# Retuning the start of a planned RWKV-5 plus tanh-shrink kernel: when weights are fetched, where the own terms are made, and how wide the idle products are

## The chip, the cores and the metric

One core of a Trainium2 chip runs the whole program. The metric is the device time of one execution in microseconds (us), the median of three runs. A TensorE product of float32 appears in the trace as two passes, each a weight load (PEld) and a multiplication (PE); a transpose is one such pair.

## The reference

```python
state = zeros((B, H, D, D))                      # B=4, H=8, S=768, D=48
for t in range(S):
    cur = einsum('bhd,bhe->bhde', u[None] * k[t], v[t])
    y[t] = einsum('bhd,bhde->bhe', r[t], state + cur)
    state = w[None, :, :, None] * state + einsum('bhd,bhe->bhde', k[t], v[t])
x = y.transpose(0, 2, 1, 3).reshape(B * S, H * D)  # 3072 x 384
h = x @ w_in                                      # 384 x 2048
out = (h - tanh(h)) @ w_out                       # 2048 x 384
```

The recurrence is an attention with a decay `w` for each channel and a bonus `u` for a token's own term. The weights come as float64 and are handed over as 64-bit integers.

## The kernel before

**Attention.** The sequence is cut into 24 units of 64 steps of two batch entries (128 rows). For a unit the kernel loads r, k and v (`fetch`), transposes r and k on TensorE (`turn`), scales them by powers of the decay (`rT`, `kT`), multiplies k by r (`levels`), keeps what lies strictly below the diagonal with a predicated copy (`x.cp`), puts the own terms on the diagonal (`x.diag`), multiplies by v (`outputs`), updates the state (`to_state`, `keep`, `decay`) and evicts the result as the input `xt` of the dense part. Two units make one block of 256 tokens.

**Own terms.** For the first `OWN` units they are made on TensorE: ScalarE scales `kT` by decay and bonus (`own_k`), TensorE multiplies (`own_levels`, 16 products), and VectorE copies the diagonal with a predicate. For all later units VectorE multiplies r by k, multiplies by the bonus `ub` and sums (`own`, the line after it, `own_sum`: 3 instructions), and ScalarE writes eight scaled unit matrices (`diagonal`).

**Dense part.** A tile of 256 hidden columns needs 6 products of 128x256 (`h`), five activations, four VectorE instructions (`g`, `c1`, `c2`, `cp`, the last named L195 in the profile) and 8 products of 128x384 (`o`). The first six blocks go through the hidden columns in four passes, so that only a quarter of the weights is needed early.

**Weights.** Each piece of 768 KB (two w_in pieces, then two w_out pieces, and so on) is loaded into a staging tile `st` and turned into float32 by five VectorE and two ScalarE instructions (`convert`, L134 to L140). w_in pieces are loaded half by SyncE (two transfers of 288 KB) and half by GpSimd's queue (two of 96 KB); a w_out piece is one transfer of 768 KB. All r, k, v loads are SyncE transfers of 96 KB in runs of 192 bytes.

**The planner.** `Plan` fixes the order of every engine's instructions before the program is built. Each task has a cost, predecessors and a due time; `forward` lays them out in time, `backward` gives latest times, and `order` tries 600 random shifts of due times and keeps what ends sooner. Three of its models matter here. Transfers share a channel (`data` is the channel time of a transfer) and land some time after it. A weight transfer (`gated`) is not issued sooner than 45 us ahead of its due time. TensorE's instructions come in blocks (`CHUNK` 256 instructions, the first bound at 192); `ASKED` instructions into a block the next one is requested, and it comes `COMES` after that, or after what is already on the channel.

**Idle products.** While TensorE would wait, `filled` works out how many products of the identity with itself fit in the planned gap, and `order` puts them into the instruction stream. They compute nothing that is used; they keep TensorE's clock up. Their number is fixed in the program, so they run even if the gap turns out shorter.

```python
plan.fill = lambda to: T.matmul(to, ident, ident, start=True, stop=True), .25
```

Of the kernel before, what the change touches and what calls it, by code (L numbers as in the profile page):

```python
# [34 lines left out]
L = 2  # L35
FIRST = 6
PASSES = 4, 4, 4, 4
OWN = 4
SWAP = 2


# [190 lines left out]
class Plan:  # L232
# [5 lines left out]


    HOP, NEAR_HOP, LANDS, LANDED, LANES, EARLY, SPARE, WARM, SLOW = 0.16, 0.06, 2.4, 1.6, 8, 45.0, 20.0, 6.0, (60.0, 3.0)  # L240
    CHUNK, CHUNK_0, ASKED, COMES = 256, 192, 55, 3.0
    BEGIN = {"PE": 1.5, "DVE": 2.2, "ACT": 1.2, "POOL": 4.3, "SP": 1.2}

    def __init__(self):
        self.tasks, self.fill, self.fills = [], None, []

    def add(self, engine, cost, run, after=(), due=1e9, data=0, gated=False, steps=0):
        t = SimpleNamespace(engine=engine, cost=cost, run=run, after=[x for x in after if x], due=due, data=data,
# [16 lines left out]

    def forward(self, due):

        ready = [due[t.n] - self.EARLY if t.gated else 0.0 for t in self.tasks]
        count = [len(t.after) for t in self.tasks]
        waiting = self.queues(ready, count)  # L270
        free, lanes, channel = dict(self.BEGIN), {}, 0.0
        step, bound, comes, fills = 0, self.CHUNK_0, 0.0, iter(self.fills)
        filling = next(fills, None)
        starts, done, last, first, changed = [None] * len(ready), [], 0.0, {}, set(waiting)
        while len(done) < len(ready):
            for e in changed:
                ts = waiting[e]
                first.pop(e, None)
                if not ts:
                    continue  # L280
                start = max(free.get(e, 0.0), min(ready[x.n] for x in ts))
                t = min((x for x in ts if ready[x.n] <= start + 1e-9), key=lambda x: (due[x.n], x.n))
                if t.data:
                    start = max(start, lanes.setdefault(e, [0.0] * self.LANES)[0])
                else:

                    soon = [x for x in ts if ready[x.n] < start + t.cost and due[x.n] < due[t.n] - self.SPARE]
                    if soon:
                        t = min(soon, key=lambda x: (ready[x.n], x.n))
                        start = max(start, ready[t.n])  # L290
                first[e] = start, t
            e = min(first, key=lambda x: (first[x][0], x))
            start, t = first[e]
            waiting[e].remove(t)
            changed = {e}
            end = start + t.cost
            if e == "PE":
                if filling:
                    step += 4 * self.filled(filling, free[e], start, starts)
                    if t is filling[1]:  # L300
                        filling = next(fills, None)
                step += t.steps
                if step >= bound:
                    each = t.cost / max(t.steps, 1)
                    crossed = end - (step - bound) * each
                    late = max(0.0, comes - crossed)
                    end += late
                    comes = max(crossed + late + self.ASKED * each + .3, channel) + self.COMES
                    bound += self.CHUNK
            free[e] = end  # L310
            if t.data:
                channel = max(channel, start + 1.2) + t.data
                end = max(end + self.LANDS, channel + self.LANDED) + self.slow(start)
                lanes[e] = lanes[e][1:] + [end]
            starts[t.n] = start
            last = max(last, end)
            done.append(t)
            for x in t.then:
                ready[x.n] = max(ready[x.n], end + self.hop(t, x))
                count[x.n] -= 1  # L320
                if not count[x.n]:
                    waiting[x.engine].append(x)
                    changed.add(x.engine)
        return last, starts, done
# [4 lines left out]

    def filled(self, filling, free, start, starts):  # L330

        after = [starts[x.n] and starts[x.n] + x.cost + self.HOP for x in filling[0]]
        if None in after:
            return 0
        return max(0, int((start - max([free] + after)) / (self.fill[1] * (2 if start < self.WARM else 1))))

    def backward(self, plan):

# [27 lines left out]
    def order(self, tries=600):  # L366


        due = [t.due for t in self.tasks]
        for t in reversed(self.tasks):  # L370
            for x in t.then:
                due[t.n] = min(due[t.n], due[x.n] - t.cost - self.HOP - (self.LANDS if t.data else 0))
        plan = self.forward(due)
        for _ in range(4):
            due = self.backward(plan)
            plan = self.forward(due)
        chance = Random(3)
        for _ in range(tries):
            by, at, wide = chance.choice((0.3, 1, 2, 5)), chance.uniform(0, plan[0]), chance.choice((15, 40, 100, 700))
            moved = [x + chance.gauss(0, by) * (abs(start - at) < wide / 2) for x, start in zip(due, plan[1])]  # L380
            other = self.forward(moved)
            if chance.random() < .5:
                latest = self.backward(other)
                again = self.forward(latest)
                if again[0] < other[0]:
                    other, moved = again, latest
            if other[0] <= plan[0]:
                plan, due = other, moved
        self.due = due
        _, starts, done = plan  # L390
        free, order, fills = self.BEGIN["PE"], [], iter(self.fills)
        filling = next(fills, None)
        for t in done:
            t.start = starts[t.n]
            if t.engine == "PE" and filling:
                n = self.filled(filling, free, t.start, starts)
                order += [SimpleNamespace(engine="PE", cost=0.0, start=free, run=lambda to=filling[2]: self.fill[0](to))] * n
                if t is filling[1]:
                    filling = next(fills, None)
                free = t.start + t.cost  # L400
            order.append(t)
        return order
# [19 lines left out]
def near(ctx, tc, r, k, v, w, u, out, shared, weights):  # L422
# [84 lines left out]
    wcol = cols_ps[:, :NP]  # L507
    saved, w_u = fixed("saved", [128, 2 * NP]), fixed("w_u", [128, NP])
    idle, tab = (ps_d.tile([128, 2, d.NT], F32, name="h", tag="h") for _ in range(2))
    idle, tab = idle[:, 0, :128], tab.rearrange("s z t -> s (z t)")  # L510
    flat = "d p n -> d (p n)"

    def bounds():
# [7 lines left out]
            T.transpose(tab[:, p * 128 : (p + 1) * 128], twice[:, p].rearrange("d z n -> d (z n)"), ident)  # L521


    plan.fill = lambda to: T.matmul(to, ident, ident, start=True, stop=True), .25  # L524

    now = [add(e, 1.25 if e == "ACT" else .87, lambda e=e, at=at, x=x: e_of[e].dma_start(out=rows[at : at + NP, :, :D], in_=x.rearrange("(p i) d -> p i d", i=2)), due=-1, data=.05)
           for e, at, x in (("SP", 0, w), ("ACT", NP, u))]
# [8 lines left out]
    ups = add("ACT", .6, lambda: A.copy(w_up, power[:, :, None, :SHORT].to_broadcast([128, NP, 2, SHORT])), [now])  # L536
    now = add("DVE", 1.75, lambda: V.reciprocal(inverse, power), [now])
    doubled = add("DVE", .4, lambda: V.tensor_copy(twice, inverse[:, :, None, 1:].to_broadcast([128, NP, 2, SHORT])), [now])
    now = add("PE", .7, table, [doubled], steps=8)
    downs = add("ACT", .5, lambda: A.copy(w_down, tab.rearrange("s (h d) -> s h d", h=H)[:, :, :D]), [now])  # L540
    keeps = add("ACT", .2, lambda: A.copy(saved, cols_ps), [cols])
    w_us = add("DVE", .1, lambda: V.tensor_tensor(w_u, saved[:, :NP], saved[:, NP:], ALU.mult), [keeps])
# [21 lines left out]
    loads, converted = [], []  # L564
    for n in range(weights.count):

        queues, data = (("SP",), (2.4,)) if n % 4 > 1 else (("SP", "POOL") * 2, (.85, .55) * 2)
        of = [add(e, .55, lambda n=n, i=i, e=e: weights.load(n, i, e_of[e]), [converted[n - 4] if n >= 4 else None],
                  data=x, gated=True) for i, (e, x) in enumerate(zip(queues, data))]
        if weights.sources[n % 4 > 1].dtype != I64:  # L570
# [17 lines left out]
    def unit(n):  # L588
# [20 lines left out]
        def fetch(name, src, after):  # L609
            def run(z):  # L610
                if name == "k" and not hasattr(t, "kt"):
                    t.kt = first_k[slot] if direct else load.tile([128, H, D], F32, name="kt", tag="kt")
                to = {"r": rt, "v": vt}.get(name)
                Q.dma_start(out=(t.kt if to is None else to)[HALF[z], :, :D],  # L614
                            in_=src[half * 2 + z, :, steps_at, :].rearrange("h t d -> t h d"))

            of = [add("SP", .65, lambda z=z: run(z), after, data=.58) for z in range(2)]
            return add("none", 0, lambda: None, of)

        x.r = fetch("r", r, [b3.turn, b3.rk, b1.r])  # L620
# [18 lines left out]

        def own():  # L640
            t.rk = work.tile([128, H, D], F32, name="rk", tag="rk")
            V.tensor_tensor(t.rk, rt[:, :, :D], t.kt, ALU.mult)

        def own_sum():
            t.du = work.tile([128, H], F32, name="du", tag="du")
# [134 lines left out]
    def hidden(j, fs, f, due, pace):  # L780
# [8 lines left out]
        x.h = add("PE", 1.29, lambda: dense.h(t, 1), [now], due + 1.3, steps=12)  # L789
        last_h[j] = x.h  # L790
        if m == 0:
            plan.fills.append(([], now, idle))
        x.s = add("ACT", .48, lambda: dense.act(t, "s"), [x.h, b2.c1, b2.q, b2.small, b1.s])
        x.th = add("ACT", .48, lambda: dense.act(t, "th"), [x.h, b2.g, b1.th])
        x.tg = add("ACT", .48, lambda: dense.act(t, "tg"), [x.h, b2.cp, b1.tg])
        x.q = add("ACT", .63, lambda: dense.act(t, "q"), [x.s, b2.c2, b1.q])
        x.small = add("ACT", .63, lambda: dense.act(t, "small"), [x.s, b2.cp, b1.small])
# [3 lines left out]
        x.cp = add("DVE", .65, lambda: dense.vec(t, "cp"), [x.c2, x.small, x.g])  # L801
        now = add("PE", 1.3, lambda: dense.o(t, 0), [x.cp, converted[piece + 2], b1.o] + b1.empty + ([units[1].cp, units[1].diag] if m == 0 else []), due + 2 * pace, steps=8)
        if m == 0:
            plan.fills.append(([units[1].cp, units[1].diag], now, x_banks[1][:, 0, :128]))
        x.o = add("PE", 1.3, lambda: dense.o(t, 1), [now], due + 2 * pace + 1.3, steps=8)
        if not t.last:
            return
# [339 lines left out]
```

## Time and profile before

| | us |
|---|---|
| median of three runs | 622.67 |
| lowest, highest | 620.96, 622.95 |
| profiled span | 621.0 |
| TensorE busy | 602.6 |
| VectorE busy | 429.9 |
| ScalarE busy | 398.5 |
| products `h` (L165) and `o` (L203), busy | 281.6 and 280.6 |
| idle products (L524), busy, into `h` and into `x_ps` | 16.2 and 3.4 |

TensorE is busy for 97% of the span, but busy time of overlapping passes is counted from start to modelled end, and idle products count as busy. A time per instruction is therefore read from start to start.

### The profile page before, as it was taken

The page shows a single profiled execution, that of the slowest core. Times are in us where ns is not written, and L with a number is a line of the kernel's source. Part 1 is how long each engine was busy: PE and PEld are TensorE (multiplying, and loading weights), DVE is VectorE, ACT ScalarE, POOL GpSimd, SP SyncE. Part 2 cuts the span into 40 slices and gives each one's busy share as a digit, 9 for nine tenths or more (in the row PEclk, how much of TensorE's full clock was granted, in tenths as well). Part 3 has the DMA queues.
Part 4 walks back from the last instruction along what each step waited for, and adds up shares of the span by engine and source line. Part 5 has one row for each costly group of instructions (what it writes and reads, how often), then busy time and mean ns, then how long its engine had stood idle before and what let it go on. Part 6 is the DMA issues. An engine that isn't in the chain of part 4 may idle for free.

```text
span 621.0 us, 13303 instructions
## 1 busy us (share of the span) xinstructions
PE 602.6 (97%) x5337; PEld 448.6 (72%) x5337; DVE 429.9 (69%) x700; ACT 398.5 (64%) x873; POOL 68.8 (11%) x153
## 2 busy tenths in 40 slices
PE   7799999999999999999999999999999999999995
PEld 6777777677777777777777777777777777777773
DVE  5699979998985797776676747475766455455552
ACT  2488879978665667555574756674774566665651
POOL 4001311300000000011132010011010101110100
PEclk9799999999999999999999999999999999999998
DMA  8976796234520000011233111211210100100101
GB/s 124 201 131 112 128 219 117 45 74 132 91 98 0 1 1 2 0 26 39 52 84 63 29 33 27 51 35 23 55 31 3 27 14 8 26 5 4 26 1 31
DMA packets 86320, 33.71 MB, mean 54 GB/s; under 512 B 78536, under 2 KB 80680, under 8 KB 86248
## 3 DMA queue, kind: packets, MB, share of 16 engines
q1 hardware_dynamic: 81084, 25.57, 21.1%
q0 software_dynamic: 4992, 6.99, 5.2%
q8 instruction: 44, 0.72, 0.5%
q10 hardware_dynamic: 172, 0.20, 0.1%
q14 instruction: 28, 0.23, 0.1%
HBM read 26.94 MB, written 4.72 MB: 51 GB/s over the span
## 4 chain that ended last, share of the span: by engine, by line
PE 84%; DVE 5%; DMA 4%; ACT 3%; issue 2%; SPq 1%; POOL 0%; POOLq 0%; DVEq 0%; ACTq 0%
PE h L165 37%; PE o L203 36%; PE yk_ps L584 5%; PE x_ps L626 3%; DMA rt<-in_r_dram 2%; PE x_ps L584 1%; PE h L524 1%; DMA xt<-rest 1%; SPq L614 1%; DVE rT L630 1%; DMA st<-in_moe_w_in_dram 1%; ACT kT L638 1%; DVE tg L193 1%; DVE g L195 1%; DVE at L761 0%
## 5 line engine op out<-in xcount | busy, mean ns | idle before, releaser
L203 PE MATMUL o<-w_out_sb,g 128*128 128x384 f32 x768 | 280.6, 489 | 1.8 <-DVE g L195 1.2
L165 PE MATMUL h<-xt,w_in_sb 128*128 128x256 f32 x1152 | 281.6, 381 | 0.0
L165 PEld LDWEIGHTS h<-xt,w_in_sb 128*128 128x128 f32 x1152 | 216.1, 190 | 62.3
L203 PEld LDWEIGHTS o<-w_out_sb,g 128*128 128x128 f32 x768 | 142.6, 190 | 65.4 <-DVE g L195 1.5
L191 DVE SCALAR_TENSOR_TENSOR tg<-s,tg 128x512 f32<-128x512 f32 x96 | 66.0, 688 | 71.0 <-ACT tg L178 44.1
L189 DVE TENSOR_TENSOR g<-h,th 128x512 f32<-128x512 f32 x96 | 65.9, 686 | 50.3 <-ACT s L174 31.7
L174 ACT ACTIVATE s<-h 128x512 f32<-128x512 f32 x96 | 57.1, 595 | 54.2 <-PE h L165 54.1
L178 ACT ACTIVATE tg<-h 128x512 f32<-128x512 f32 x96 | 57.0, 594 | 53.7 <-PE h L165 53.6
L176 ACT ACTIVATE th<-h 128x512 f32<-128x512 f32 x96 | 57.3, 597 | 38.6 <-PE h L165 38.6
L195 DVE COPY_PREDICATED g<-small,tg 128x512 f32<-128x512 int32 x96 | 70.4, 734 | 5.6
L193 DVE SCALAR_TENSOR_TENSOR tg<-q,tg 128x512 f32<-128x512 f32 x96 | 65.9, 686 | 7.2 <-ACT q L180 4.4
L180 ACT ACTIVATE q<-s,m1b 128x512 f32<-128x512 f32 x96 | 69.7, 726 | 0.5
L182 ACT ACTIVATE small<-s,smallb 128x512 f32<-128x512 f32 x96 | 69.6, 725 | 0.1
L726 POOL DMA_DIRECT2D xt<-rest x66 | 32.2, 495 | 202.1 <-ACT rest L712 201.3
L650 ACT ACTIVATE at<-same,du 128x64 f32<-128x64 f32 x160 | 41.3, 339 | 0.4
L226 POOL DMA_DIRECT2D out_dram<-part x24 | 12.5, 527 | 157.8 <-DVE part L211 157.8
L630 DVE TENSOR_TENSOR rT<-x_ps,w_up 128x512 f32<-128x512 f32 x24 | 16.5, 689 | 16.8 <-ACT kT L638 10.4
L638 ACT COPY kT<-x_ps 128x512 f32<-128x512 f32 x22 | 12.9, 587 | 20.3 <-PE x_ps L626 14.7
L211 DVE TENSOR_TENSOR part<-o,part 128x384 f32<-128x384 f32 x36 | 19.8, 549 | 6.4 <-PE o L203 6.4
L584 PEld LDWEIGHTS yk_ps<-at,vt 64*64 64x64 f32 x752 | 13.4, 137 | 11.2 <-issue 4.4
L226 POOL DMA_DIRECT2D out_dram<-o x20 | 10.6, 533 | 95.7 <-ACT o L220 95.5
L524 PE MATMUL h<-ident 128*128 128x128 f32 x90 | 16.2, 336 | 4.8 <-issue 3.3
(96 smaller groups left out, 442.0 us busy)
## 6 DMA issues: line engine op xcount, KB each, us to landing
st<-in_moe_w_out_dram SPq DMA_DIRECT2D x8, 768.0 KB, 10.6
rt<-in_r_dram SPq DMA_DIRECT2D x48, 96.0 KB, 3.5
vt<-in_v_dram SPq DMA_DIRECT2D x48, 96.0 KB, 3.1
st<-in_moe_w_in_dram SPq DMA_DIRECT2D x16, 288.0 KB, 5.4
kt<-in_k_dram SPq DMA_DIRECT2D x44, 96.0 KB, 3.3
out_dram<-part POOLq DMA_DIRECT2D x24, 96.0 KB, 2.2
out_dram<-o POOLq DMA_DIRECT2D x20, 96.0 KB, 2.1
st<-in_moe_w_in_dram POOLq DMA_DIRECT2D x16, 96.0 KB, 4.6
```

The costliest lines, as they stand in the source:

```text
L165: self.nc.tensor.matmul(t.h2[:, z], self.w_in_sb[:, t.f // 2, kk, z * 128 : (z + 1) * 128], self.xts[t.j][:, kk].rearrange("p b t -> p (b ...
L174: A.activation(out, t.h, AF.Square)
L176: A.activation(out, t.h, AF.Tanh)
L178: A.activation(out, t.h, AF.Tanh, scale=G1)
L180: A.activation(out, t.s, AF.Square, bias=self.m1b)
L182: A.activation(out, t.s, AF.Relu, bias=self.smallb, scale=-1.0)
L189: V.tensor_tensor(t.g, t.h, t.th, ALU.subtract)
L191: V.scalar_tensor_tensor(t.tg, t.s, C4, t.tg, ALU.mult, ALU.mult)
L193: V.scalar_tensor_tensor(t.tg, t.q, K1, t.tg, ALU.add, ALU.mult)
L195: V.copy_predicated(t.g, t.small.bitcast(I32), t.tg)
L203: self.nc.tensor.matmul(self.outs[i], t.g2[:, z, i * C : (i + 1) * C], self.w_out_sb[:, t.f + z, :], start=t.first and z == 0, stop=t.last ...
L584: T.matmul(*args, skip_group_check=True, **how)
```

## The change

It has four parts. (1) `FIRST` = 9.5: weight transfers are planned no sooner than 9.5 us, which puts them behind the loads of the first two units. (2) The planner gets larger figures for transfers and for the arrival of an instruction block. (3) `OWN` goes from 4 to 1: only the first unit has its own terms made on TensorE. (4) An idle gap is filled with 128x512 products (`ident` by the decay powers `w_up`) as far as they fit and with 128x128 ones for the rest; those need `w_up`, so a first stretch of narrow ones up to the task `tabled` is kept. The other edits follow from these: `first_k` tiles are wider than 48 columns, hence the slice in `own`, and they share their buffers with `th`, hence the two extra predecessors of `x.th`.

```diff
-OWN = 4
+OWN = 1
-    CHUNK, CHUNK_0, ASKED, COMES = 256, 192, 55, 3.0
+    CHUNK, CHUNK_0, ASKED, COMES, FIRST = 256, 192, 55, 3.4, 9.5
-        ready = [due[t.n] - self.EARLY if t.gated else 0.0 for t in self.tasks]
+        ready = [max(self.FIRST, due[t.n] - self.EARLY) if t.gated else 0.0 for t in self.tasks]
-                    step += 4 * self.filled(filling, free[e], start, starts)
+                    step += 4 * len(self.filled(filling, free[e], start, starts))
-        return max(0, int((start - max([free] + after)) / (self.fill[1] * (2 if start < self.WARM else 1))))
+        runs = []
+        for cost, run in filling[2]:
+            n = max(0, int((start - free) / (cost * (2 if start < self.WARM else 1))))
+            free += n * cost
+            runs += [run] * n
+        return runs
...
-    plan.fill = lambda to: T.matmul(to, ident, ident, start=True, stop=True), .25
+    def fills(to):
+        wide = w_up.rearrange("d p z t -> d (p z t)")
+        return [(.9, lambda: T.matmul(to, ident, wide, start=True, stop=True)),
+                (.25, lambda: T.matmul(to[:, :128], ident, ident, start=True, stop=True))]
...
-        queues, data = (("SP",), (2.4,)) if n % 4 > 1 else (("SP", "POOL") * 2, (.85, .55) * 2)
+        queues, data = (("SP",), (3.0,)) if n % 4 > 1 else (("SP", "POOL") * 2, (1.2, .8) * 2)
-            of = [add("SP", .65, lambda z=z: run(z), after, data=.58) for z in range(2)]
+            of = [add("SP", .65, lambda z=z: run(z), after, data=.62) for z in range(2)]
-            V.tensor_tensor(t.rk, rt[:, :, :D], t.kt, ALU.mult)
+            V.tensor_tensor(t.rk, rt[:, :, :D], t.kt[:, :, :D], ALU.mult)
-            plan.fills.append(([], now, idle))
+            plan.fills += [([], tabled, fills(idle)[1:]), ([ups], now, fills(idle))]
-        x.th = add("ACT", .48, lambda: dense.act(t, "th"), [x.h, b2.g, b1.th])
+        x.th = add("ACT", .48, lambda: dense.act(t, "th"), [x.h, b2.g, b1.th] + ([units[m].rk, units[m].kw] if m < L else []))
-            plan.fills.append(([units[1].cp, units[1].diag], now, x_banks[1][:, 0, :128]))
+            plan.fills.append(([units[1].cp, units[1].diag], now, fills(x_banks[1][:, 0])))
```

What the planner makes of it at the start, engine by engine. SyncE: before, the order was r, k, v of the first unit, one w_in transfer, r and k of the second, two w_in, v of the second, w_in, w_out, then r and k of the third and the bonus; now k, r, v of the first unit, the bonus, k, r and half of v of the second, two w_in, the rest of v, k and r of the third, two w_in, w_out. GpSimd's four w_in transfers, which stood ahead of its first copy out of `v`, now stand behind it. TensorE: the transpose of the second unit's k now precedes the first unit's own-term product, where it followed the first unit's outputs. Between the second unit's `levels` and the first `o` product there stand 11 wide and 9 narrow idle products, where there were 18 narrow into `h` and 12 narrow into `x2_ps`. The `levels` of the fifth unit now stand ahead of the first `o`. VectorE and ScalarE: 3 VectorE and 8 ScalarE instructions for the own terms of units two, three and four each, in place of one and four. The second w_out piece is loaded later, between the halves of the v of the sixth unit, where it stood ahead of the v of the third. Over the whole program the changes between `h` and `o` are about as many as before (304 against 309).

More of the change, by code (lines that the diff above doesn't have):

```diff
@@ L240 @@
     HOP, NEAR_HOP, LANDS, LANDED, LANES, EARLY, SPARE, WARM, SLOW = 0.16, 0.06, 2.4, 1.6, 8, 45.0, 20.0, 6.0, (60.0, 3.0)
-    CHUNK, CHUNK_0, ASKED, COMES = 256, 192, 55, 3.0
+    CHUNK, CHUNK_0, ASKED, COMES, FIRST = 256, 192, 55, 3.4, 9.5
     BEGIN = {"PE": 1.5, "DVE": 2.2, "ACT": 1.2, "POOL": 4.3, "SP": 1.2}
     def __init__(self):
-        self.tasks, self.fill, self.fills = [], None, []
+        self.tasks, self.fills = [], []
     def add(self, engine, cost, run, after=(), due=1e9, data=0, gated=False, steps=0):
@@ L330, in filled @@
     def filled(self, filling, free, start, starts):
-        after = [starts[x.n] and starts[x.n] + x.cost + self.HOP for x in filling[0]]
-        if None in after:
-            return 0
-        return max(0, int((start - max([free] + after)) / (self.fill[1] * (2 if start < self.WARM else 1))))
+        for x in filling[0]:
+            if starts[x.n] is None:
+                return []
+            free = max(free, starts[x.n] + x.cost + self.HOP)
+        runs = []
[4 more added lines that the diff above has]
+        return runs
     def backward(self, plan):
@@ L395, in order @@
             if t.engine == "PE" and filling:
-                n = self.filled(filling, free, t.start, starts)
-                order += [SimpleNamespace(engine="PE", cost=0.0, start=free, run=lambda to=filling[2]: self.fill[0](to))] * n
+                order += [SimpleNamespace(engine="PE", cost=0.0, start=free, run=run)
+                          for run in self.filled(filling, free, t.start, starts)]
                 if t is filling[1]:
@@ L509, in near @@
     idle, tab = (ps_d.tile([128, 2, d.NT], F32, name="h", tag="h") for _ in range(2))
-    idle, tab = idle[:, 0, :128], tab.rearrange("s z t -> s (z t)")
+    idle, tab = idle.rearrange("d z t -> d (z t)"), tab.rearrange("s z t -> s (z t)")
     flat = "d p n -> d (p n)"
@@ L538, in near @@
     doubled = add("DVE", .4, lambda: V.tensor_copy(twice, inverse[:, :, None, 1:].to_broadcast([128, NP, 2, SHORT])), [now])
-    now = add("PE", .7, table, [doubled], steps=8)
+    now = tabled = add("PE", .7, table, [doubled], steps=8)
     downs = add("ACT", .5, lambda: A.copy(w_down, tab.rearrange("s (h d) -> s h d", h=H)[:, :, :D]), [now])
```

## The prediction

> **What bounds the kernel now.** I read the page first, then busy time by stretch, then TensorE's and VectorE's timelines of the first 60 us, then the chain of waits. The page, parts 1 and 2:
>
> ```profile
> PE 602.6 (97%) x5337; PEld 448.6 (72%) x5337; DVE 429.9 (69%) x700; ACT 398.5 (64%) x873; POOL 68.8 (11%) x153
> PE   7799999999999999999999999999999999999995
> DVE  5699979998985797776676747475766455455552
> PEclk9799999999999999999999999999999999999998
> DMA  8976796234520000011233111211210100100101
> ```
>
> From about 50 us on TensorE never rests, and no part of the change touches that work. So the question is when this steady stretch begins. The clock falls below full only in the second slice (15.5 to 31 us), and there the DMA engines are full. Busy time by stretch (PE, PEld, DVE, ACT, POOL, then the clock, the DMA share and GB/s):
>
> ```profile
> 10.00:15.00 5.00, 2.98 (x76) 2.46 (x76) 2.41 (x7) 1.64 (x5) 0.26 (x1) 1.00 1.25 167
> 15.00:20.00 5.00, 3.47 (x95) 2.85 (x93) 2.64 (x5) 1.75 (x5) 0.00 (x0) 1.00 1.18 157
> 25.00:30.00 5.00, 5.00 (x93) 4.72 (x94) 4.95 (x7) 1.34 (x3) 0.00 (x0) 0.56 0.75 184
> 50.00:60.00 10.00, 9.21 (x167) 6.72 (x170) 9.87 (x18) 7.39 (x25) 2.93 (x6) 1.00 0.56 106
> ```
>
> Until 20 us TensorE and VectorE are half idle and the DMA share is above 1; later VectorE is full. TensorE's timeline (start, length, instruction, in brackets the idle time before it and who ended it) shows the stops:
>
> ```profile
> 14.59 0.63 PE L626 MATMUL x_ps<-ident,rt 128*128 128x128 f32 x4 [1.40 <-DMA rt<-in_r_dram]
> 17.20 1.27 PE L524 MATMUL h<-ident 128*128 128x128 f32 x9
> 21.73 0.38 PE L524 MATMUL h<-ident 128*128 128x128 f32 x1 [3.26 <-issue]
> 51.11 1.53 PE L203 MATMUL o<-w_out_sb,g 128*128 128x384 f32 x4 [0.79 <-DVE g L195]
> ```
>
> The second unit's r lands at 14.5. At 18.47 TensorE stops for 3.26 us in the middle of idle products that wait for nothing: 220 passes, or 440 instructions, have run, and an instruction block is missing. The first `o` at 51.11 is my landmark: behind it TensorE is nearly dense. VectorE's two waits for w_in:
>
> ```profile
> 17.92 0.56 DVE L134 TENSOR_SCALAR power<-st 128x768 uint32<-128x768 uint32 x1 [1.62 <-DMA st<-in_moe_w_in_dram]
> 23.76 0.56 DVE L134 TENSOR_SCALAR power<-st 128x768 uint32<-128x768 uint32 x1 [3.15 <-DMA st<-in_moe_w_in_dram]
> ```
>
> From 23.76 to 50.98, where the last instruction ahead of the landmark (L195) ends, VectorE has under 3 us of gaps.
>
> [...] Here the clock reads 0.50 from 23 to 29 us, after the 3.26 us stop. [...]
>
> **The change, part by part.**
>
> *Weights behind the first loads.* SyncE issues one 96 KB transfer each 0.65 us. Without w_in between, and with the bonus instead, the second unit's r is issued by 9.5 (k, r, v by 6.2 as now, the bonus 0.65, k 1.3, r 1.3). The first unit's r took 2.7 us from issue (3.5) to its transpose (6.25), so r is there at about 12.3, 2.2 us sooner. The price is w_in: the first piece now follows 1.25 MB of loads (k, r, v, bonus, k, r, half a v); with itself (768 KB) and GpSimd's share of the second (192 KB) that is 2.2 MB. The windows of before moved 0.17, 0.85 and 0.84 MB in the first three stretches of 5 us and then 157 GB/s: 2.2 MB at 17.2, at worst 18.8 by the pace at which before's own pieces landed. So the first conversion starts about when it did (17.92).
>
> *The instruction block.* Ahead of the second unit's `levels` 211 passes now run instead of 220, so the same bound falls nine passes into them. Before it took 7.1 us from r's transpose (14.59) to resumption (21.73), and the request seems to hang on about that place. From 12.4 this gives 18.7 to 19.5; I take 19.2. The stop remains, as long as before (idle from 15.6), but 2.5 us earlier.
>
> *Idle products.* No 128x512 product is in the trace. A pass of 256 columns takes 0.215 us start to start (1.29 for six), so two of 512 take 0.86 at full clock, 1.72 at half. These are the two bounds; I take the first with part of the second. A narrow one takes 0.24. From 19.2 to the landmark TensorE then has 11 wide (9.5), 9 narrow (2.2), the rest of `levels` (0.4), six groups of transposes (2.8), outputs and states of units two to four (3.3), `levels` of three to five (3.1) and two tiles of `h` (5.2): 26.5, ending at 45.7. Gaps in which it waits for data were 2.0 between 32 and 51 us (0.16, 0.19, 0.88, 0.79); the same again gives 47.7.
>
> *Own terms.* TensorE loses 3 x 32 passes, 0.52 us each unit, 1.6 in all, all ahead of the landmark. VectorE pays three instructions of 0.47 in place of one of 0.62: 0.8 a unit, 2.4 in all; ScalarE pays 2.0 in place of 1.2. VectorE is the full engine there, so this is on the path: its instructions from the first conversion to the last one of the first tile's `g` now sum to 26.9 us (start to start: 0.47 at 384 columns and for L134 and L135, 0.87 for the other conversions, 0.60 to 0.62 at 512 columns). From 17.2 to 18.8 that is 44.1 to 45.7 without a wait. But the third unit's k and r are 2.7 MB down the line, at 20.3 by the same pace plus up to 1.6 to land, and VectorE reaches them at 18.1 (one conversion pair in): 2 to 3 us, then about 1 us in all on the second w_in, w_out and the fourth unit's k, which come just as they are needed. Result 47.5 to 49.5.
>
> *Sum.* Both engines point to a first `o` at about 48.5: 2.6 earlier. The fifth unit's `levels` (0.62 + 0.47) are done by then: 1.1. Behind the landmark the work is the same. VectorE has a stretch there (`o` of the second block) in which its summed work equals TensorE's, where before it had 3.5 us of slack; 0.3 for that. 622.67 - 2.6 - 1.1 + 0.3 = 619.3.
>
> The larger transfer figures only change the order, counted above. The extra predecessors of `th` cost nothing: the own multiplications of the second unit and the `kw` of both end by about 17, `th` runs after `h`, beyond 25. The tail is unchanged.
>
> **Rivals.**
> - *The clock halves again.* The stop is as long as before. At half clock for 7 us the fixed wide products stretch: 3.5 us are lost, part of it in gaps. The landmark comes at 50.5 to 51: 622.67 - 0.4 - 1.1 + 0.2 = 621.4. For it: the same 3.3 us of idleness. Against: [...] the three times of before already spread by 2 us.
> - *The waits vanish.* The block comes earlier on a less mixed queue and the loads keep up, so that VectorE is full from 17.2 with 1 us of gaps: landmark at 45.1, 622.67 - 6.0 - 1.1 = 615.6. For it: idle time of 9.7 us on VectorE ahead of 51 us, which is there to be had. Against: the DMA share above 1.
> - *Slower.* The own terms on VectorE and late w_in meet a half clock, and the next block, requested behind slow wide products, stops the third unit's `levels` for 2 us more: landmark at 53, and 1 us lost to VectorE behind it: 622.67 + 1.9 - 1.1 + 1.0 = 624.5. For it: VectorE at 9.87 of 10. Against: TensorE sheds work and r comes earlier.
>
> **How the numbers follow.** My forecast has a chance of 0.5 (617.5 to 620.8), the clock 0.24, vanishing waits 0.16, slower 0.10. Faster by over 0.3% means below 620.8: the forecast's 0.47, all of the vanishing waits and 0.07 of the clock make 0.70. Within 0.3% (to 624.5): 0.03, 0.16 and 0.02 make 0.21; slower 0.09. The range 615.8 to 622.5 leaves out half of the vanishing waits and nearly all of the slower case, with the edges of the clock case.
>
> **What would show it.** Right: r's transpose near 12.4; an issue wait of about 3 us in the second unit's `levels`, ending near 19; the first L134 between 17 and 19; the first `o` between 47.5 and 49.5; and from there the same length to the end but for 1.1. A clock of 0.5 after 20 us with a landmark at 51 speaks for the first rival, no issue wait and a landmark at 45 for the second. Wrong altogether: a landmark as forecast, and a steady stretch longer by more than 2 us.

## The result and the profile after

| | before | after |
|---|---|---|
| median, us | 622.56 | 620.21 |
| lowest to highest, us | 620.96 to 622.95 | 619.64 to 621.25 |
| profiled span, us | 621.0 | 617.9 |
| first `o`, us | 51.11 | 51.36 |
| issue stop of TensorE, us | 3.26, ending at 21.73 | 4.44, ending at 20.95 |

The ratio after to before is 0.9969, with a 95% interval of [0.9947, 0.9991] (four runs of each). The change saves 2.3 us, near the 619.3 that was forecast. But the first `o`, the landmark, which was to come 2.6 us earlier, comes 0.25 us later. The total was right and the way to it was not: that the sum came out is in part luck.

The page of the changed kernel, parts 1 and 2:

```profile
PE 601.9 (97%) x5211; PEld 444.5 (72%) x5211; DVE 433.2 (70%) x706; ACT 401.8 (65%) x885; POOL 69.8 (11%) x153
...
PE   8799999999999999999999999999999999999995
...
DVE  6699977999689857996676665757556655555552
...
PEclk9899999999999999999999999999999999999999
DMA  6974446953006200001241221221101000100101
```

Little stands out: 126 TensorE passes fewer, VectorE busy 3.3 us longer, the same two thin slices at the start. Busy time by stretch of the changed kernel (PE, PEld, DVE, ACT, POOL, then the clock, the DMA share and GB/s) shows more:

```profile
10.00:15.00 5.00, 4.46 (x145) 3.73 (x148) 4.14 (x10) 1.64 (x5) 1.63 (x4) 1.00 0.94 185
15.00:20.00 5.00, 1.44 (x42) 1.05 (x33) 3.55 (x9) 3.69 (x11) 0.29 (x1) 1.00 1.26 159
20.00:25.00 5.00, 4.05 (x28) 2.14 (x29) 3.63 (x6) 0.89 (x2) 0.00 (x0) 0.66 0.91 162
25.00:30.00 5.00, 5.00 (x99) 3.46 (x97) 2.81 (x6) 1.96 (x6) 0.00 (x0) 1.00 1.05 243
50.00:60.00 10.00, 9.63 (x220) 7.46 (x220) 10.00 (x19) 6.27 (x18) 2.34 (x5) 1.00 0.40 77
```

Ahead of 15 us TensorE now does much more (4.46 busy in place of 2.98). The five microseconds behind are nearly empty, with the DMA share at 1.26. The clock is lower for one short stretch: 0.66 over 5 us is 3.4 us at half speed (1.6 + 3.4 x 0.5 = 3.3 of 5). Before, it was at half for 6.8 us (0.81 and 0.78 in the microseconds from 22 and 29, 0.50 between). From 50 us on VectorE is full. TensorE's timeline of the changed kernel:

```profile
13.22 0.66 PE L636 MATMUL x_ps<-ident,rt 128*128 128x128 f32 x4
...
16.13 0.38 PE L594 MATMUL x_ps<-rT,kT 48*64 48x64 f32 x9
20.95 0.87 PE L594 MATMUL x_ps<-rT,kT 48*64 48x64 f32 x23 [4.44 <-issue]
21.75 4.18 PE L532 MATMUL h<-w_up,ident 128*128 128x512 f32 x6
...
26.65 0.60 PE L636 MATMUL x_ps<-ident,rt 128*128 128x128 f32 x4
...
51.36 1.88 PE L203 MATMUL o<-w_out_sb,g 128*128 128x384 f32 x5
```

The stop falls nine passes into the second unit's `levels`, the place that was forecast, but lasts 4.44 us. Six wide passes then take 4.18 us, largely at half clock, and the third unit's r is turned only at 26.65. VectorE's waits in the changed kernel:

```profile
18.59 0.56 DVE L134 TENSOR_SCALAR power<-st 128x768 uint32<-128x768 uint32 x1 [1.08 <-DMA st<-in_moe_w_in_dram]
...
21.37 0.56 DVE L750 TENSOR_TENSOR kw<-kt,w_down 128x384 f32<-128x384 f32 x1 [1.75 <-DMA kt<-in_k_dram]
...
27.96 0.69 DVE L640 TENSOR_TENSOR rT<-x_ps,w_up 128x512 f32<-128x512 f32 x1 [2.19 <-ACT kT L648]
...
31.70 0.75 DVE L771 COPY_PREDICATED at<-before,x_ps 128x512 f32<-128x512 int32 x1 [0.78 <-PE x_ps L594]
```

From the copy at 31.70 to the first `o` VectorE has hardly a gap; in this order of instructions, that full stretch of 19.7 us sets the landmark.

Where, then, did the time come from? The two executions that were profiled lie 3.1 us apart (spans 621.0 and 617.9), more than the medians, because that of the changed kernel is the fastest of its four. I used a sum by stretches. Each pass of use is priced by an estimate from its length start to start in the dense part (0.2155 us for one of `h`, 0.3225 for `o`, 0.01625 for a 64-wide one of the attention, 0.113 for a transpose). The length of a stretch minus that sum is lost time; own-term passes and idle products count as lost.

| lost, us | 0 to 60 | 60 to 130 | 130 to 400 | 400 to last `o` | sum |
|---|---|---|---|---|---|
| before | 34.2 | 4.8 | 3.7 | 4.4 | 47.2 |
| after | 33.3 | 3.5 | 3.0 | 5.1 | 44.9 |

The last `o` ends 2.3 us earlier (611.72 against 614.03), and what follows it is 0.8 us shorter (6.2 against 7.0). Of the 2.3, the start gives only 0.9: by 60 us the changed kernel has 26.7 us of useful work behind it, before 25.8. That is what the landmark says too, once the fifth unit's `levels`, now ahead of it, are counted (1.1 gained, 0.25 lost). From the landmark to the end the changed kernel takes 566.5 us, before 569.9: 3.4 less, where the forecast had only those 1.1, less 0.3. This sum is of one execution each, and what saved the rest is not shown.

### The profile page after: what moved, and what is told of

The parts are those of the page before. It is cut to its first block, busy times and chain, and to the rows that moved or that the text cites. A ratio compares the mean times of both kernels' runs of the same rounds, so it can differ in the third digit from the quotient of the medians.

```text
span 617.9 us, 13049 instructions
## 1 busy us (share of the span) xinstructions
PE 601.9 (97%) x5211; PEld 444.5 (72%) x5211; DVE 433.2 (70%) x706; ACT 401.8 (65%) x885; POOL 69.8 (11%) x153
## 4 chain that ended last, share of the span: by engine, by line
PE 89%; DVE 5%; issue 2%; ACT 1%; DMA 1%; SPq 0%; POOL 0%; DVEq 0%; ACTq 0%; POOLq 0%
PE h L165 39%; PE o L203 38%; PE yk_ps L594 5%; PE x_ps L636 3%; PE x_ps L594 2%; PE h L533 1%; DMA rt<-in_r_dram 1%; PE h L532 1%; DVE rT L640 1%; DVE tg L193 1%; DVE rk L652 0%; DVE tg L191 0%; DMA vt<-in_v_dram 0%; DVE g L189 0%; DVE g L195 0%
## 5 line engine op out<-in xcount | busy, mean ns | idle before, releaser
L660 ACT ACTIVATE at<-same,du 128x64 f32<-128x64 f32 x184 | 47.8, 341 | 0.6 <-DVE du L656 0.3
L226 POOL DMA_DIRECT2D out_dram<-part x24 | 12.5, 526 | 125.3 <-DVE part L211 125.3
L720 ACT COPY xt<-yk_ps 128x192 f32<-128x192 f32 x22 | 7.1, 321 | 28.0 <-PE yk_ps L594 28.0
L771 DVE COPY_PREDICATED at<-before,x_ps 128x512 f32<-128x512 int32 x24 | 17.5, 728 | 4.5 <-PE x_ps L594 4.2
L594 PE MATMUL x_ps<-rT,kT 48*64 48x64 f32 x768 | 16.2, 221 | 4.6 <-issue 4.4
```

Source lines behind the costliest of these rows:

```text
L594: T.matmul(*args, skip_group_check=True, **how)
```

## The experiments

The change moves the order on every engine, so two kinds of experiment were needed. Some keep the changed kernel's order and alter only idle products. The others put back, or make, one part and are planned again; for these I had to know what another draw of the planner's random search does by itself.

### One part put back, planned again

**Own terms of four units on TensorE** (`a_own4`).

```diff
-OWN = 1
+OWN = 4
```

> The changed kernel with OWN back at 4, planned anew: own terms of units two to four on TensorE again. If the own terms on VectorE are a price (2.4 us of a full engine ahead of the first o), this is as fast as the changed kernel or up to 1.5 us faster: 618.7 to 620.2, first o before 50. If taking them off TensorE is what brought the gain (1.6 us of TensorE work), it is slower: 621.5 to 622.5.

Measured: 626.94 us, 1.0071 [1.0051, 1.0092] of before, so 6.7 us above the changed kernel and above both of the outcomes that I had named. The stop in the issue is 5.35 us long. This kernel is the slowest of all, and its first `o` comes at 49.32, two microseconds ahead of the changed kernel's.

**No gate on the weights** (`a_first0`).

```diff
-    CHUNK, CHUNK_0, ASKED, COMES, FIRST = 256, 192, 55, 3.4, 9.5
+    CHUNK, CHUNK_0, ASKED, COMES, FIRST = 256, 192, 55, 3.4, 0.0
```

> The changed kernel without the bound of 9.5 us for weight transfers, planned anew with the larger transfer figures. If holding the weights back brings the gain, 622 or more. If it is worth nothing because the larger figures alone already put the loads first, 619.5 to 621.

Measured: 619.42 us, 0.9964 [0.9951, 0.9976]. Taking the bound away costs nothing. But it does not put the weights first again. SyncE's transfers in before:

```profile
6.26 0.62 SPq L120 DMA_DIRECT2D st<-in_moe_w_in_dram  x1
6.93 1.28 SPq L614 DMA_DIRECT2D rt<-in_r_dram  x2
8.25 1.31 SPq L614 DMA_DIRECT2D first_k<-in_k_dram  x2
```

In the changed kernel:

```profile
8.26 1.31 SPq L624 DMA_DIRECT2D rt<-in_r_dram  x2
9.61 0.63 SPq L624 DMA_DIRECT2D vt<-in_v_dram  x1
10.29 1.10 SPq L120 DMA_DIRECT2D st<-in_moe_w_in_dram  x2
```

In this one:

```profile
7.87 1.31 SPq L624 DMA_DIRECT2D first_k<-in_k_dram  x2
9.23 3.17 SPq L120 DMA_DIRECT2D st<-in_moe_w_in_dram  x3
```

Without the bound the planner still puts SyncE's first w_in transfer behind the second unit's r and k, which before did not. Only GpSimd's four transfers go out early again, from 5.36 us on, where the changed kernel has them from 9.45. TensorE's timeline of this kernel:

```profile
16.15 1.88 PE L532 MATMUL h<-w_up,ident 128*128 128x512 f32 x4
17.87 0.50 PE L533 MATMUL h<-ident 128*128 128x128 f32 x3
18.90 0.60 PE L533 MATMUL h<-ident 128*128 128x128 f32 x3 [0.54 <-issue]
19.43 0.69 PE L594 MATMUL x_ps<-rT,kT 48*64 48x64 f32 x32
```

The stop is 0.54 us, and the clock stays at full speed (1.00 in every stretch up to 600 us). Wide idle products, four passes of which last 1.72 us from start to start, stand ahead of it, but that alone doesn't explain it: this kernel gets there at 18.36 us, before got there at 18.47 and stopped for 3.26. What differs is the end of the stop: TensorE goes on at 18.90 in place of 21.73. Why it goes on sooner is not shown. This kernel's lost time at the start is the lowest of all (30.3 us), yet it loses 6.4 us behind 400 us, against 5.1.

**Narrow idle products only** (`a_narrow`).

```diff
-        return [(.9, lambda: T.matmul(to, ident, wide, start=True, stop=True)),
+        return [(1e9, None),
```

> The changed kernel with narrow idle products alone, planned anew. A wide product takes as much time as three and a half narrow ones and a quarter of the instructions for it. If the arrival of instruction blocks binds the start, narrow ones bring further stops: 621.5 to 623. If only the time of the idle products counts, no change: 619.5 to 621.

Measured: 621.22 us, 0.9986 [0.9974, 0.9997], between the two outcomes that I had named; a stop of 4.76 us and 6.8 us of half clock. (A wide pass takes 0.43 us from start to start and a narrow one 0.13 in `a_first0`, at 16.15 and 21.88 us.)

**The former figures for transfers and fetch** (`a_oldfig`).

```diff
-    CHUNK, CHUNK_0, ASKED, COMES, FIRST = 256, 192, 55, 3.4, 9.5
+    CHUNK, CHUNK_0, ASKED, COMES, FIRST = 256, 192, 55, 3.0, 9.5
...
-        queues, data = (("SP",), (3.0,)) if n % 4 > 1 else (("SP", "POOL") * 2, (1.2, .8) * 2)
+        queues, data = (("SP",), (2.4,)) if n % 4 > 1 else (("SP", "POOL") * 2, (.85, .55) * 2)
...
-            of = [add("SP", .65, lambda z=z: run(z), after, data=.62) for z in range(2)]
+            of = [add("SP", .65, lambda z=z: run(z), after, data=.58) for z in range(2)]
```

> The changed kernel with the old figures for transfers and block arrival, planned anew. If the truer figures make the plan fit the chip, this is slower by 1 to 2 us: 621 to 622.5, with more idle time of TensorE before the first o. If they do not matter, 619.5 to 621.

Measured: 623.61 us, 1.0023 [1.0013, 1.0034], above both of the outcomes that I had named.

### The scatter of the search

**Another seed**, of before (`b_seed`) and of the changed kernel (`a_seed`).

```diff
-        chance = Random(3)
+        chance = Random(4)
```

> The kernel before with another seed of the planner's random search, nothing else. If the orders that the search finds are worth much the same, 621.5 to 623 with the same loss in every stretch. If the gain of the change could be luck of one order, it moves by more than 1.5 us either way.

> The changed kernel with the same other seed, nothing else. If the gain is that of the change, 619 to 621. If it is luck of one order, it moves by more than 1.5 us from 620.2, and the places where TensorE loses time move with it.

Measured: before's code with seed 4 takes 623.80 us, 1.0031 [1.0015, 1.0046] of before; the changed code takes 624.42, 1.0047 [1.0032, 1.0062]. So 4.2 us lie between two draws of the same code, more than the change gained, and from seed 4 the changed code is no faster than the old one. Figures and wide products, each put back once, moved the time by 3.4 and 1.0: no more than a draw can.

**The missing gate from the other seed** (`a_first0_seed`): both edits together.

> The changed kernel without the gate of 9.5 us on weight transfers, planned again from another seed (4 in place of 3). With seed 3 this variant took 619.42 us, stopped for 0.54 us only and kept the clock at full speed. If that comes from the missing gate, the stop is again under 1.5 us and the time 618.5 to 620.5. If it was one draw of the random search, the stop of 3 to 5 us with a half clock is back and the time is 621 to 625, as with the two other kernels whose seed was changed (623.8 and 624.4).

Measured: 622.29 us, 1.0008 [0.9998, 1.0018]. TensorE's timeline has the stop again:

```profile
16.89 0.61 PE L594 MATMUL yk_ps<-vt,kw 64*64 64x48 f32 x27
21.07 0.46 PE L594 MATMUL yk_ps<-vt,kw 64*64 64x48 f32 x5 [3.57 <-issue]
```

So the short stop was the luck of one draw, not the missing gate. The gate itself brought no gain in two pairs: 619.42 without and 620.21 with it, 622.29 without and 624.42 with it. Here too SyncE's first w_in goes out only at 9.39 us, behind the loads of two units. What that order is worth, neither pair can say.

### Idle products, with the order kept

**Without the five idle products behind the second unit's `levels`** (`a_nogap`). `gap` counts the planned gaps that get idle products; the seventh is this one.

```diff
...
-                order += [SimpleNamespace(engine="PE", cost=0.0, start=free, run=run)
-                          for run in self.filled(filling, free, t.start, starts)]
+                runs = self.filled(filling, free, t.start, starts)
+                gap += bool(runs)
+                order += [SimpleNamespace(engine="PE", cost=0.0, start=free, run=run) for run in ([] if gap == 7 else runs)]
```

> The changed kernel in the same order, without the three wide and two narrow idle products that follow the second unit's levels. If fixed idle products hold up the third unit's transposes (they ran from 21.75 to 26.2, while its k was there at 21.4), these come at 22.5 to 23, VectorE's rT at 25.7 in place of 27.96, the first o at about 49.2 in place of 51.36, and the time is 618 to 618.5. If the clock then stays at half because TensorE has too little to do, the gain is spent: 620 or more.

Measured: 621.53 us, 1.0002 [0.9983, 1.0021]. Its TensorE timeline:

```profile
21.11 0.92 PE L595 MATMUL x_ps<-rT,kT 48*64 48x64 f32 x23 [4.99 <-issue]
...
23.18 1.06 PE L637 MATMUL x_ps<-ident,rt 128*128 128x128 f32 x4
...
28.69 0.44 PE L595 MATMUL yk_ps<-rT,state 48*64 48x64 f32 x11
29.87 0.51 PE L595 MATMUL yk_ps<-rT,state 48*64 48x64 f32 x19 [0.74 <-issue]
...
50.66 2.85 PE L203 MATMUL o<-w_out_sb,g 128*128 128x384 f32 x8
```

The third unit's r is turned 3.5 us earlier, and 2.8 of these are gone by the first `o`, which gains 0.7, while the time is 1.3 us longer than the changed kernel's. Four transposes take 1.06 us here in place of 0.60: the clock is at half for 6.8 us in place of 3.4. And the next block of instructions, now also reached sooner, is not there: a stop of 0.74.

**Without any idle product from there to the first `o`** (`a_nofill`): the same edit with `gap >= 7`.

> The changed kernel in the same order, without any idle product between the second unit's levels and the first o. If they are only a cost by then, 617.5 to 618.5, first o at 48.5 to 49. If they keep the clock up as they are meant to, it falls to half in the gaps of 30 to 50 us, real products take twice as long there, and the time is 621 or more.

Measured: 625.15 us, 1.0051 [1.0032, 1.0071]. Its TensorE timeline:

```profile
45.44 1.13 PE L595 MATMUL yk_ps<-at,vt 64*64 64x64 f32 x32 [3.08 <-DVE at L772]
...
52.61 1.13 PE L595 MATMUL yk_ps<-rT,state 48*64 48x64 f32 x32 [3.65 <-DVE state L743]
```

TensorE waits for VectorE (3.08 and 3.65 us), and behind each wait 32 passes take 1.13 us, where the same in this kernel take 0.69 at full clock (at 36.25 and 41.10 us): 1.6 times as long, not twice. The clock is at half from 21.2 to 34.8, from 45.1 to 48.5 and from 51.9 to 58.7 us, 23.9 us in all, where the changed kernel has 3.4. The useless products of this stretch are worth 5 us (625.15 against 620.21).

**Fewer instructions ahead of the stop** (`a_early`).

```diff
...
+                runs = self.filled(filling, free, t.start, starts)
+                gap += bool(runs)
+                if gap < 7:
+                    runs = [self.broad] * ((len(runs) + 1) // 4) or runs
...
+    def broad(to):
+        return lambda: T.matmul(to, ident, ident[:, None, :].to_broadcast([128, 4, 128]), start=True, stop=True)
```

> The changed kernel in its own order, but the narrow idle products ahead of the table product and just behind it are replaced by a quarter as many of 128x512 (the identity by itself, repeated four times): 28 passes, 56 instructions, fewer ahead of the second unit's levels, for about the same time. If the stop of TensorE is a missing instruction block (a bound after 220 passes), levels of the second unit runs through before 17.5 us and the stop falls five passes into the wide idle products behind it, from about 18 to about 21.5 us; VectorE's copies of that unit then no longer wait for TensorE, the third unit's r is turned by 23.5 (changed kernel 26.65), the first o comes at 48.5 to 50, and the time is 618.5 to 619.8 us. If something else stops TensorE (a buffer or data of levels that the trace does not show), the stop stays nine passes into levels and the time at 620.2. If the start is not what decides the total, the first o moves but the time stays within 0.5 us of 620.2.

Measured: 620.43 us, 0.9971 [0.9961, 0.9982], the same as the changed kernel. Its TensorE timeline:

```profile
16.29 0.69 PE L600 MATMUL x_ps<-rT,kT 48*64 48x64 f32 x32
16.92 2.41 PE L535 MATMUL h<-w_up,ident 128*128 128x512 f32 x5
22.29 0.70 PE L535 MATMUL h<-w_up,ident 128*128 128x512 f32 x1 [2.96 <-issue]
...
24.08 0.63 PE L642 MATMUL x_ps<-ident,rt 128*128 128x128 f32 x4 [0.22 <-DMA rt<-in_r_dram]
...
28.02 0.68 PE L600 MATMUL yk_ps<-rT,state 48*64 48x64 f32 x29
30.33 0.27 PE L600 MATMUL yk_ps<-rT,state 48*64 48x64 f32 x2 [1.63 <-issue]
...
52.27 2.85 PE L203 MATMUL o<-w_out_sb,g 128*128 128x384 f32 x8
```

`levels` runs through and the stop falls five passes into the wide products, to the pass as the count of instructions says. The third unit's r is turned 2.6 us earlier. Nothing of it reaches the end, and VectorE's timeline of this kernel says why:

```profile
22.59 0.56 DVE L756 TENSOR_TENSOR kw<-kt,w_down 128x384 f32<-128x384 f32 x1 [2.95 <-DMA kt<-in_k_dram]
...
31.41 0.73 DVE L777 COPY_PREDICATED at<-before,x_ps 128x512 f32<-128x512 int32 x1 [1.27 <-PE x_ps L600]
```

VectorE's first wait is for the third unit's k, whatever TensorE does (2.95 us in place of 1.75). Its second is for the third unit's `levels`, behind the next missing block (the stop of 1.63 us). The copy at 31.70 in the changed kernel starts at 31.41: 0.3 us are left of the 2.6. Behind that stop the clock is at half for 3.4 us (0.66 over 30 to 35 us), VectorE has three more short gaps, and the first `o` comes at 52.27, 0.9 us later than in the changed kernel, for the same time in all.

### Own terms put into the kernel before

**From two seeds** (`b_own1`, `b_own1_seed`); the slice in `own` and the two predecessors of `th` go with it.

```diff
-OWN = 4
+OWN = 1
```

> The kernel before with one part of the change alone: own terms on TensorE for the first unit only (and the two edits that this needs), planned again. 96 passes of own terms fall away ahead of the first o, 1.6 us of TensorE, against 2.4 us more of VectorE. If the removed passes are what the change gained, the first o is within 1 us of before's 51.1, the length behind it shrinks, and the time is 620.5 to 621.7. If the new order that the search finds weighs more, the time lies anywhere from 619 to 625, with a stop in the issue of 3 to 5 us, and this run settles nothing about the part.

> The kernel before with own terms on TensorE for the first unit only, planned from another seed (4). Pairs so far: with seed 3, before 621.9 and this edit 619.8; with the figures and products of the changed kernel and seed 3, 626.9 with four units and 620.2 with one. If the removed 96 passes (1.6 us of TensorE) are what gains, this run is at least 1 us below before's order from the same seed (623.8): 620.5 to 622.8. If both pairs were draws of the search, it lies anywhere from 620 to 626, and one at or above 623.8 would show a draw outweighing the part.

Measured: 619.80 us, 0.9967 [0.9957, 0.9977] of before, and from seed 4 619.44, 0.9952 [0.9937, 0.9966], where the old code from seed 4 has 1.0031. The first is below what I expected of it (620.5 to 621.7), and its first `o` is 2.3 us later than before's, where I had allowed one. TensorE's timeline of `b_own1`:

```profile
52.12 1.46 PE L165 MATMUL h<-xt,w_in_sb 128*128 128x256 f32 x6
53.42 1.45 PE L203 MATMUL o<-w_out_sb,g 128*128 128x384 f32 x4
```

A further `h` tile stands ahead of the first `o`: it comes later because more has been done. The three pairs whose code differs in own terms alone, each planned for itself:

| planner's figures, idle products, gate | four units on TensorE: us, first `o` | one unit: us, first `o` |
|---|---|---|
| of before, seed 3 | 621.87, 51.11 | 619.80, 53.42 |
| of before, seed 4 | 623.80, 47.17 | 619.44, 55.16 |
| of after, seed 3 | 626.94, 49.32 | 620.21, 51.36 |

All three pairs gain, 2.1, 4.4 and 6.7 us. In all three the first `o` comes later. The code differs in own terms alone, but the planned order doesn't: in the first two pairs the planner also moves SyncE's first w_in behind the second unit's r and k (from 6.26 to 9.62 us, and from 6.25 to 9.23), so part of these two gains may be that order's. In the third pair it goes out at 10.29 in both. In the first pair the lost time of 0 to 60 us falls from 34.2 to 32.2, in the third from 38.0 to 33.3; the 96 passes themselves, which count as lost, are 96 x 0.01625 = 1.56 us. (The profiled execution of `b_own1_seed` took 621.75 us, above its median, so its trace is not summed here.)

## Why the prediction was right, and where it was not

*The clock.* It was said to fall below full in the second slice alone. The page's last digit, 8, says that it also falls in the last slice, behind the final products; nothing hung on that.

*The second unit's r at 12.4.* It is turned at 13.22. The load is not what held it: the first unit's k is now turned ahead of its r, which moved that r from 6.25 to 8.25 us and the own-term product of the first unit from 11.7 to 12.5; the turn stands behind that product in TensorE's order.

*The stop: nine passes into `levels`, 3.3 us, resuming at 19.2.* The place was exact. The length was 4.44 and the end 20.95, 7.7 us from r's turn in place of the 7.1 that I had carried over. Over the draws the stop took from 0.5 to 5.4 us; its length is what the profile of before could not give.

*Wide products at near full clock.* Six passes took 4.18 us; at the 0.43 us from start to start that four at full clock take in `a_first0`, they would be 2.6, an estimate. The rival of a halving clock came true in part: 3.4 us of it, not 7.

*VectorE: first conversion at 17.2 to 18.8, a wait of 2 to 3 us for k and r.* It starts at 18.59 and waits 1.75. But the 2.19 us behind TensorE's late turns, put down to ScalarE's `kT`, which follows them, were not in the sum.

*The first `o` at 48.5, 2.6 us earlier.* Wrong: 51.36, by the two errors above. `a_early` and `a_nogap` show that even turning r 2.6 and 3.5 us earlier would not have brought it: waits for k, a slower clock and the next instruction block took its place.

*Behind the landmark the work is the same.* This is the step that failed. It made the first `o` the measure of the whole, on the ground that TensorE is dense behind it. But the planner chooses what stands ahead of the landmark, and the three pairs show it moving against the total each time. With the order kept it is no better: `a_nogap` has it 0.7 us earlier and is 1.3 us slower, `a_early` has it 0.9 us later and is as fast. How much useful work is done by a fixed time says more; there the start gained 0.9 us, where 3.7 were forecast, and the rest came behind 60 us, where I had put a loss of 0.3. One error made up for the other, which is luck. What the gain behind 60 us is due to stays open: two draws of the changed code lie 4.2 us apart, more than this gain.

*Own terms: TensorE -1.6, VectorE +2.4 on the path.* The sizes are right, and VectorE is indeed full from 31.70 to the landmark. The weight of the two seems to have been wrong. In all three pairs the kernel with less on TensorE is faster by at least the 1.6 us, though its first `o` comes later. That fits TensorE having the least slack over the whole program (busy for 97% of it, with the idle products counted, VectorE for 70%). This part, which I had costed as more of a price than a gain at the start, is the only one that gained in every pair; made alone in the code before it gives all that the whole change gives (0.9967 against 0.9969).

*Weights behind the first loads*, from which I had most of the gain, remain untested: the bound brought nothing in two pairs, but the order was much the same without it, and no kernel with one unit on TensorE has w_in ahead. The larger figures and the wide products can't be told from the scatter of the search: each was tried from one seed only, and that stays open. Taken together, gate, figures and wide products can be read from three pairs that have the same number of own terms on TensorE:

| units on TensorE, seed | code before, apart from own terms: us | with gate, figures and wide products: us |
|---|---|---|
| one unit, seed 3 | 619.80 | 620.21 |
| one unit, seed 4 | 619.44 | 624.42 |
| four units, seed 3 | 621.87 | 626.94 |

In none of the three do they gain. From seed 4, where own terms gain 4.4 us, they lose it again, and the whole change is no faster than the code before. How far all these differences are the parts' own and how far they are draws stays open: two draws of the same code lie up to 4.2 us apart. No kernel tried is faster than the changed one by more than the intervals allow; the nearest are `a_first0` and `b_own1_seed`.

## What to carry to other kernels

Where an order is planned anew after each edit, don't take one instruction's start as the measure of progress: sum the useful work done by a fixed time. Plan each version from several seeds before an edit of a few tenths of a per cent is credited with anything; here one seed to the next was 4 us and the change 2.3. Taking work from the engine with the least slack in the whole program went with a gain in three pairs of three, even though the engine that got it was full for the stretch in question. When one part is taken out and the plan is made again, look whether the order that the part was to bring has gone with it: here it had not.

## What the runs showed of the hardware

**TensorE's first stop in the issue comes at a counted place.** By the records it comes after exactly 220 passes in all fourteen kernels, whatever stands there: idle products in before, `levels` in the changed kernel, wide products in `a_early`, where 28 passes had been taken out ahead. A second comes 126 passes on in `a_nogap`, `a_nofill`, `a_early` and `a_seed`. That is 252 instructions of weight load and multiplication, near the 256 that the planner takes for a block (`CHUNK`). That an instruction block is missing is read from this count and from the instruction queue q8: in before its only packet between 12 and 24 us is seen at 18 to 18.5, and the stop lasts from 18.47 to 21.73; in the changed kernel its only one between 12 and 26 us is seen at 18 to 18.5 too, and the stop lasts from 16.51 to 20.95. The first stop took from 0.54 us (`a_first0`) to 5.35 (`a_own4`); the DMA share from 15 to 20 us was 1.26 in the changed kernel and 1.18 in before and in `a_first0`, so it doesn't say how long. Thirty-two 64-wide passes go by in 0.52 us (0.01625 each); as many passes of a 128x512 product, at the 0.43 us each of `a_first0`, would take some 14, an estimate. So what a stretch is filled with decides how soon the next such place is reached.

**The length of a stretch at half clock doesn't follow the length of the stop.** In the first 60 us stretches at half clock of three lengths are seen: 3.4 us (as in the changed kernel and `a_early`), 6.8 us (as in before, `a_narrow` and `a_nogap`) and, once, 13.7 us (`a_nofill`); `a_first0` has none. The length of the stop doesn't say which: 6.8 us went with a stop of 2.26 us in `a_oldfig` and of 4.99 in `a_nogap`, 3.4 us with one of 4.44 in the changed kernel. Nor does it say whether the clock falls: in `a_early` it stayed full behind a stop of 2.96 us (1.00 over 20 to 30 us) and fell to half behind one of 1.63. What decides it is not shown.
